# A Fourier filter and a soft mixture of experts on one core: the first DFT stage folded into sums and differences of token pairs, on quarters of PE

## The chip, the cores and the metric

The kernel runs on one core of a Trainium2 chip. The metric is the device time of one execution in microseconds (us). The engines are PE (matrix products; PEld is its weight load), DVE, ACT and POOL (elementwise work; ACT also functions) and SP, which here issues nearly all DMAs. All arrays are float32. float32r is a reduced form of float32 in which a product makes fewer passes over PE.

## The reference

`x` has 8 batches of 2496 tokens and 256 channels. Each batch is filtered along the tokens, and the result goes through a soft mixture of 8 experts with 4 slots each.

```
X = np.fft.rfft(x, axis=1);  Y = X * (filt_r + 1j * filt_i)
x = np.fft.irfft(Y, n=2496, axis=1).reshape(19968, 256)
logits = x @ phi                                   # 19968 x 32 slots
d = softmax of logits over the tokens;  slot_input = d.T @ x
slot_out[e] = relu(slot_input[e] @ w1[e]) @ w2[e]  # 8 experts, 256 -> 1024 -> 256
c = softmax of logits over the slots;   out = c @ slot_out
```

## The kernel before

The DFT of length 2496 = 39 x 64 is done by two smaller ones. A token is `(64*s + 39*k) mod 2496`, with s from 0 to 38 and k from 0 to 63. The **first stage** is the real DFT of length 39 over s, for every k. Of it 20 cosine rows and 20 sine rows are kept. The **second stage** is a complex DFT of length 64 over k, for each of the 20 frequencies.

The host lays x out so that three k stand on the partitions at a time: 3 x 39 = 117 rows, and 22 columns of three k. A *unit* (`b`, `u`) of the first stage is two of those columns, 512 numbers a row; a batch has 11 units. `split_x` makes a rounded copy of the unit (`xh`, a cast to float32r on ACT, line 310) and what the rounding left (`xl`, a subtraction on POOL, line 311). `s1_unit` forms three float32r products on the whole array, `xh` with the rounded weights `w1h`, `xh` with the weights' rest `w1l`, and `xl` with `w1h` (line 327), 120 rows out of 117. ACT copies the result to `at` (line 331), and SP writes `at` to `a_dram` in DRAM (line 284). Batch 0 goes another way (`b < FB`): one float32 product a unit (line 323), without a split.

`load_ash` reads `a_dram` back with k on the partitions, two frequencies at a time (`ash`, 256 KB); a batch's first `ash` needs all of its writes. The main loop has 80 slots, one for each batch and pair of frequencies `c`. In a slot `x_unit` forms the second stage (line 357, `x`), DVE multiplies by the filter `ff_t` (lines 371 and 372) and adds, with POOL, into `yt` (lines 374 and 375). Two slots later `t_unit` transposes `yt` (line 383, `t`), ACT copies it to `y` (line 385), and after each second slot eight products with phi on 32 columns of PE give `l` (line 394). For groups of one or two batches `chain` runs beside the slots: the inverse DFT of the logits, maxima, exponentials, and the sums over tokens (lines 414 to 616; `s` of line 417 is the sum over tokens, `lg` the logits). After the last slot come the rest of the chains, the experts (lines 910 to 939) and the output (lines 966 to 985).

The units of batches 1 to 7 are spread over the slots: `slot_of` gives each its slot, `split_next` splits one slot ahead and asks for the next part of x (`next_x`, three buffers `xt`), and the first `EARLY` units of batch 1 run before the loop. Within these rules a scheduler fixes the order of instructions on each engine at build time. Each engine runs its own in that order. DMAs from `issue` keep the order of the code up to slot `PIN`.

Of the kernel before, what the change touches and what calls it, by code (L numbers as in the profile page):

```python
# [19 lines left out]
NT = 20  # L20
# [28 lines left out]
AB = 5  # L49
EARLY = 4  # L50
# [10 lines left out]
FIRST = (0, 2, 6, 10, 14, 18, 22)  # L61
# [23 lines left out]
def shape_constants():  # L85
# [46 lines left out]
    put("m1", inverse(b1))  # L132
    put("bh", bh.reshape(P, P))
# [60 lines left out]
def token_layout(x):  # L194

    n = np.array([[[token_of(s, min(PK * i + j, N2 - 1)) for i in range(NI)] for s in range(N1)] for j in range(PK)])
    rows = np.zeros((BATCH, P, NI, DIM), x.dtype)
    rows[:, 0:KR] = x[:, n.reshape(KR, NI)]
    return rows
# [26 lines left out]
def fft_soft_moe(ctx, tc, x, ff, phi, wx, cst, w1q, out):  # L226
# [73 lines left out]

    def split_x(b, u):

        if b < FB:
            xhl[b, u] = x0_t[0:KR, 2 * u : 2 * u + 2, :], None
            return
        c, k = divmod(2 * u, XC)
        xs = xts[b, c][0:KR, k : k + 2, :]
        xh = proda.tile([KR, 2, DIM], F32R, tag="xh", name=f"xh{b}_{u}", bufs=3)
        xl = proda.tile([KR, 2, DIM], F32R, tag="xl", name=f"xl{b}_{u}", bufs=3)
        act.copy(xh, xs)  # L310
        pool_e.tensor_tensor(out=xl, in0=xs, in1=xh.bitcast(F32), op=ALU.subtract)  # L311
        xhl[b, u] = xh, xl
# [3 lines left out]
    def s1_unit(b, u):  # L316
        if u == 0:
            a_dram[b] = scr.tile([N2, QR, DIM], F32, tag="a_dram", name=f"a_dram{b}")
        xh, xl = xhl.pop((b, u))
        ps = ps_s1.tile([QP, 2, DIM], F32, tag="s1", name=f"s1_{b}_{u}")  # L320
        if xl is None:
            at = ypool.tile([QP, 2, DIM], F32, tag="y", name=f"at{b}_{u}")
            behind("pe", pe.matmul(ps, w1q_t, xh, start=True, stop=True))
        else:
            at = proda.tile([QP, 2, DIM], F32, tag="at", name=f"at{b}_{u}", bufs=AB)
            for n, (w, xx) in enumerate(((w1h, xh), (w1l, xh), (w1h, xl))):
                pe.matmul(ps, w, xx, start=(n == 0), stop=(n == 2))  # L327
        if b == 0 and u % 2 == 1:
            dve.tensor_copy(at, ps)
        else:  # L330
            act.copy(at, ps)  # L331
# [682 lines left out]
```

## Time and profile before

| | |
|---|---|
| median of 3 runs | 400.98 us (396.01, 400.98, 401.02) |
| profiled execution | 398.26 us, its span 396.3 us, mean granted PE clock 0.96 |
| busy share of the span | PE 91%, PEld 70%, DVE 67%, ACT 54%, POOL 51% |
| DMA | 109.08 MB, mean 275 GB/s |
| first x product | 27.87 us |
| last copy of the first stage | 227.7 us |
| last x product | 287.5 us |
| experts, output | from 322.5 us; from 341.2 us to the end |

In the profile a group of instructions is named by its line, engine, operation and tiles (`out<-in`), with buffer numbers left out. A float32 product on PE leaves two records, a float32r product or a transpose one. A record's length contains the time in which the next one has already begun, so the pace of PE is read from one start to the next. A row such as `117*120 117x512` means 117 rows and 120 columns of PE in use, and 512 columns streamed. The chain of work that ended last goes 61% of its way over PE, 15% over DVE and 13% over DMAs.

### The profile page before, as it was taken

The page shows a single profiled execution, that of the slowest core. Times are in us where ns is not written, and L with a number is a line of the kernel's source. Part 1 is how long each engine was busy: PE and PEld are TensorE (multiplying, and loading weights), DVE is VectorE, ACT ScalarE, POOL GpSimd, SP SyncE. Part 2 cuts the span into 40 slices and gives each one's busy share as a digit, 9 for nine tenths or more (in the row PEclk, how much of TensorE's full clock was granted, in tenths as well). Part 3 has the DMA queues.
Part 4 walks back from the last instruction along what each step waited for, and adds up shares of the span by engine and source line. Part 5 has one row for each costly group of instructions (what it writes and reads, how often), then busy time and mean ns, then how long its engine had stood idle before and what let it go on. Part 6 is the DMA issues. An engine that isn't in the chain of part 4 may idle for free.

```text
span 396.3 us, 11436 instructions
## 1 busy us (share of the span) xinstructions
PE 362.1 (91%) x4569; PEld 278.9 (70%) x4569; DVE 264.2 (67%) x460; ACT 212.6 (54%) x453; POOL 200.8 (51%) x229
## 2 busy tenths in 40 slices
PE   8967889999999999999998999999999899999960
PEld 2455767887878776887887778888767544777850
DVE  1215998779789973967899355899644653588640
ACT  2356656675666946665675634347235431577430
POOL 0157688797668674856774615663421112361000
PEclk9999999999999999999998999999999999999555
DMA  8999999899889866976897783454529998299997
GB/s 293 316 291 368 395 374 373 288 318 341 261 274 305 288 212 207 291 250 171 283 328 215 200 271 104 130 147 134 170 70 380 364 249 278 111 413 421 418 414 296
DMA packets 54010, 109.08 MB, mean 275 GB/s; under 512 B 5362, under 2 KB 25970, under 8 KB 51782
## 3 DMA queue, kind: packets, MB, share of 16 engines
q1 hardware_dynamic: 53412, 108.01, 80.5%
q8 instruction: 36, 0.59, 0.6%
q10 hardware_dynamic: 546, 0.35, 0.3%
q14 instruction: 16, 0.13, 0.1%
HBM read 65.60 MB, written 42.74 MB: 273 GB/s over the span
## 4 chain that ended last, share of the span: by engine, by line
PE 61%; DVE 15%; DMA 13%; ACT 3%; issue 3%; POOL 2%; SPq 1%; DVEq 0%; ACTq 0%; POOLq 0%
PE x L357 14%; PE s L327 9%; PE t L383 7%; DMA out<-ob 5%; PE l L394 4%; PE s L417 4%; DMA ff_t<-in_ff 3%; DMA xt<-in_x 3%; PE v L417 3%; PE dd L417 2%; DVE t L372 2%; PE u L417 2%; PE lg L417 2%; DVE yt L371 2%; DVE yt L374 2%
## 5 line engine op out<-in xcount | busy, mean ns | idle before, releaser
L311 POOL TENSOR_TENSOR xl<-xt,xh 117x512 fp32r<-117x512 f32 x77 | 104.4, 1367 | 37.6 <-ACT xh L310 35.5
L357 PE MATMUL x<-cst_t,ash 128*128 128x128 f32 x640 | 90.2, 281 | 2.9 <-issue 2.3
L357 PEld LDWEIGHTS x<-cst_t,ash 128*128 128x128 f32 x640 | 81.6, 192 | 13.3 <-issue 7.5
L375 POOL TENSOR_TENSOR yt<-yt,t 128x256 f32<-128x256 f32 x80 | 65.4, 818 | 45.5 <-DVE t L372 35.9
L371 DVE TENSOR_TENSOR yt<-x,ff_t 128x512 f32<-128x512 f32 x80 | 54.7, 683 | 27.4 <-PE x L357 25.3
L385 ACT COPY y<-t 128x512 f32<-128x512 f32 x80 | 46.1, 591 | 35.5 <-PE t L383 33.2
L331 ACT COPY at<-s 120x512 f32<-120x512 f32 x83 | 48.5, 587 | 26.2 <-PE s L327 15.1
L310 ACT CAST xh<-xt 117x512 fp32r<-117x512 f32 x77 | 46.3, 623 | 23.4 <-PE s L327 12.6
L372 DVE TENSOR_TENSOR t<-x,ff_t 128x512 f32<-128x512 f32 x80 | 54.2, 678 | 0.0
L383 PE MATMUL t<-cst_t,yt 128*128 128x128 f32 x320 | 48.8, 277 | 4.8 <-POOL yt L375 4.1
L374 DVE TENSOR_TENSOR yt<-yt,t 128x256 f32<-128x256 f32 x60 | 45.3, 766 | 0.8
L383 PEld LDWEIGHTS t<-cst_t,yt 128*128 128x128 f32 x320 | 36.7, 141 | 12.7 <-POOL yt L375 7.2
L327 PE MATMUL s<-xh,w1h 117*120 117x512 f32 x77 | 35.9, 466 | 3.3 <-ACT at L331 2.1
L966 PE MATMUL out<-so,st 32*128 32x256 f32 x468 | 35.6, 337 | 2.0 <-ACT ob L971 1.0
L966 PEld LDWEIGHTS out<-so,st 32*128 32x128 f32 x468 | 30.7, 222 | 6.2 <-ACT ob L971 3.1
L327 PE MATMUL s<-xl,w1h 117*120 117x512 f32 x77 | 31.7, 416 | 0.3 <-POOL xl L311 0.3
L374 POOL TENSOR_TENSOR yt<-yt,t 128x256 f32<-128x256 f32 x20 | 15.1, 754 | 32.6 <-DVE t L372 19.9
L971 DVE COPY ob<-out 128x512 f32<-128x512 f32 (+1 forms) x40 | 25.0, 669 | 8.5 <-DMA out<-ob 5.5
L327 PE MATMUL s<-xh,w1l 117*120 117x512 f32 x77 | 30.4, 395 | 0.0
L971 ACT COPY ob<-out 128x512 f32<-128x512 f32 (+1 forms) x40 | 21.7, 583 | 14.8 <-DMA out<-ob 7.5
L394 PE MATMUL l<-yt,phi_t 128*32 128x128 f32 x640 | 27.5, 280 | 0.1
L394 PEld LDWEIGHTS l<-yt,phi_t 128*32 128x32 f32 x640 | 15.8, 109 | 9.1 <-issue 4.5
(107 smaller groups left out, 474.0 us busy)
## 6 DMA issues: line engine op xcount, KB each, us to landing
ash<-a_dram SPq DMA_DIRECT2D x80, 256.0 KB
a_dram<-at SPq DMA_DIRECT2D x80, 240.0 KB
xt<-in_x SPq DMA_DIRECT2D x35, 512.0 KB
out<-ob SPq DMA_DIRECT2D x17, 1024.0 KB
w<-in_wx SPq DMA_DIRECT2D x42, 256.0 KB
w<-in_wx SPq DMA_DIRECT2D x6, 512.0 KB
x_t<-in_x SPq DMA_DIRECT2D x5, 512.0 KB
ff_t<-in_ff SPq DMA_DIRECT2D x10, 256.0 KB
```

The costliest lines, as they stand in the source:

```text
L311: pool_e.tensor_tensor(out=xl, in0=xs, in1=xh.bitcast(F32), op=ALU.subtract)
L327: pe.matmul(ps, w, xx, start=(n == 0), stop=(n == 2))
L331: act.copy(at, ps)
L357: pe.matmul(ps[:, 2 * k + dh].rearrange("q r c -> q (r c)"), ash[:, k, dh * P : (dh + 1) * P], C("b1" if t0 + k else "b0"), start=True, st ...
L371: dve.tensor_tensor(out=yt, in0=ps, in1=frv, op=ALU.mult)
L372: dve.tensor_tensor(out=t2, in0=ps[:, :, ::-1, :], in1=fiv, op=ALU.mult)
L374: add.tensor_tensor(out=yt[:, :, 1, :], in0=yt[:, :, 1, :], in1=t2[:, :, 1, :], op=ALU.add)
L375: pool_e.tensor_tensor(out=yt[:, :, 0, :], in0=yt[:, :, 0, :], in1=t2[:, :, 0, :], op=ALU.subtract)
L383: pe.transpose(pt[:, k, dh, :], yt[:, c % 2, 2 * k + dh].rearrange("q r c -> q (r c)"), ident)
L394: pe.matmul(pl[32 * j : 32 * j + 32, :], phi_t[:, dh, :], yt[:, j // 2, 2 * (j % 2) + dh].rearrange("q r c -> q (r c)"), start=(dh == 0), ...
L417: line(pe.matmul(*a, **k))
L966: nc.tensor.matmul(prs[k][:, mm, :], sts[n][q, hs, c0 : c0 + P], so[q, ho], start=(i == 0), stop=(i == 2))
```

## The change

Cosine is even and sine odd in s, so the first stage is now done on sums and differences of the tokens s and 39 - s. The host lays x out in pairs: 20 values of s (the first stands alone), three k, two halves of the partitions (`r`), 64 rows each. The 11 units of a batch are taken in six pieces (`PIECE`): the first unit alone, then two at a time. `fold_x` makes the sums (`eo[:, 0]`, on DVE for even pieces and on POOL for odd ones; on DVE for all of batch 0) and the differences (`eo[:, 1]`, on POOL). `s1_unit` forms four float32 products on quarters of PE, 64 rows by 64 columns: cosines from the sums to columns 0 to 63, sines from the differences to columns 64 to 127, for each half of the rows, into two PSUM tiles. Two copies bring them to `at`. Each piece is written with two DMAs of 60 rows (four in the last piece). `a_dram` has the cosine and sine part outside k, so the second stage's constant has its rows in another order (`a1`). Batch 0 uses the same path, with PSUM tiles of three pools in turn and a `keep_warm` product behind pieces 3 and 4. `EARLY` is now 5 (three pieces), `AB` 4, and x is fetched after every piece.

```diff
-AB = 5
-EARLY = 4
+AB = 4
+EARLY = 5
+PIECE = ((0, 1), (1, 3), (3, 5), (5, 7), (7, 9), (9, 11))
+NU = len(PIECE)
+HR = 20
...
-    k = (b - 1) * NH + u - EARLY
+    k = (b - 1) * NH + PIECE[u][1] - 1 - EARLY
...
-    w1q_t = const.tile([KR, QP], F32, name="w1q_t")
-    act.dma_start(w1q_t, w1q)
-    w1h = const.tile([KR, QP], F32R, name="w1h")
-    w1l = const.tile([KR, QP], F32R, name="w1l")
-    nc.vector.tensor_copy(w1h, w1q_t)
-    nc.vector.tensor_tensor(out=w1l, in0=w1q_t, in1=w1h.bitcast(F32), op=ALU.subtract)
+    w1q_t = const.tile([P, 2, 64], F32, name="w1q_t")
+    act.dma_start(w1q_t.rearrange("q c m -> q (c m)"), w1q)
...
-    def keep_warm(n):
+    def keep_warm(n, w=512):
         for k in range(n):
-            behind("pe", pe.matmul(pw, warm[:, 0:P], warm, start=True, stop=True))
+            behind("pe", pe.matmul(pw[:, 0:w], warm[:, 0:P], warm[:, 0:w], start=True, stop=True))
     def load_x(b, c):
-        t = proda.tile([P, XC, DIM], F32, tag="xt", name=f"xt{b}_{c}", bufs=XB)
-        i0 = c * XC
-        n = min(XC, NI - i0)
-        issue(t[:, 0:n, :], x[b, :, i0 : i0 + n, :])
+        t = proda.tile([P, 2, 2, DIM], F32, tag="xt", name=f"xt{b}_{c}", bufs=XB)
+        lo, hi = PIECE[c]
+        issue(t[:, 0 : hi - lo].rearrange("q u a d -> q (u a) d"), x[b, :, 2 * lo : 2 * hi, :])
         xts[b, c] = t
-    xhl = {}
-    def split_x(b, u):
-        if b < FB:
-            xhl[b, u] = x0_t[0:KR, 2 * u : 2 * u + 2, :], None
-            return
-        c, k = divmod(2 * u, XC)
-        xs = xts[b, c][0:KR, k : k + 2, :]
-        xh = proda.tile([KR, 2, DIM], F32R, tag="xh", name=f"xh{b}_{u}", bufs=3)
-        xl = proda.tile([KR, 2, DIM], F32R, tag="xl", name=f"xl{b}_{u}", bufs=3)
-        act.copy(xh, xs)
-        pool_e.tensor_tensor(out=xl, in0=xs, in1=xh.bitcast(F32), op=ALU.subtract)
-        xhl[b, u] = xh, xl
+    eos = {}
+    def fold_x(b, u):
+        lo, hi = PIECE[u]
+        n = hi - lo
+        xs = x0_t[:, lo:hi] if b < FB else xts.pop((b, u))[:, 0:n]
+        eo = proda.tile([P, 2, 2, DIM], F32, tag="eo", name=f"eo{b}_{u}", bufs=2)
+        first = dve if b < FB or u % 2 == 0 else pool_e
+        first.tensor_tensor(out=eo[:, 0, 0:n], in0=xs[:, :, 0], in1=xs[:, :, 1], op=ALU.add)
+        pool_e.tensor_tensor(out=eo[:, 1, 0:n], in0=xs[:, :, 0], in1=xs[:, :, 1], op=ALU.subtract)
+        eos[b, u] = eo
     a_dram = {}
     def s1_unit(b, u):
         if u == 0:
-            a_dram[b] = scr.tile([N2, QR, DIM], F32, tag="a_dram", name=f"a_dram{b}")
-        xh, xl = xhl.pop((b, u))
-        ps = ps_s1.tile([QP, 2, DIM], F32, tag="s1", name=f"s1_{b}_{u}")
-        if xl is None:
-            at = ypool.tile([QP, 2, DIM], F32, tag="y", name=f"at{b}_{u}")
-            behind("pe", pe.matmul(ps, w1q_t, xh, start=True, stop=True))
-        else:
-            at = proda.tile([QP, 2, DIM], F32, tag="at", name=f"at{b}_{u}", bufs=AB)
-            for n, (w, xx) in enumerate(((w1h, xh), (w1l, xh), (w1h, xl))):
-                pe.matmul(ps, w, xx, start=(n == 0), stop=(n == 2))
-        if b == 0 and u % 2 == 1:
-            dve.tensor_copy(at, ps)
-        else:
-            act.copy(at, ps)
-        k0 = PK * 2 * u
-        if u < NH - 1:
-            issue(a_dram[b][k0 : k0 + 2 * PK].rearrange("(i j) q d -> (j q) i d", j=PK), at)
-        else:
-            issue(a_dram[b][k0 : k0 + PK].rearrange("j q d -> (j q) d"), at[:, 0, :])
-            issue(a_dram[b][k0 + PK], at[0:QR, 1, :])
+            a_dram[b] = scr.tile([2, N2, NT, DIM], F32, tag="a_dram", name=f"a_dram{b}")
+        lo, hi = PIECE[u]
+        n = hi - lo
+        eo = eos.pop((b, u))
+        pool, tag = ((ps_s1, "s1"), (ps_x, "x"), (ps_t, "t"))[u % 3 if b < FB else 0]
+        pss = [pool.tile([P, 2, DIM], F32, tag=tag, name=f"s1_{b}_{u}_{r}") for r in range(2)]
+        if b >= FB:
+            queue.pop("four", None)
+        for c in (1, 0):
+            for r in (1, 0):
+                q = slice(64 * r, 64 * r + 64)
+                ins = pe.matmul(pss[r][64 * c : 64 * c + 64, 0:n], w1q_t[q, c], eo[q, c, 0:n], start=True, stop=True)
+                behind("pe" if b < FB else "four", ins)
+        at = proda.tile([P, 2, 2, DIM], F32, tag="at", name=f"at{b}_{u}", bufs=AB)
+        for r in range(2):
+            copy = dve.tensor_copy if b < FB and u % 2 and r else act.copy
+            copy(at[:, 0:n, r], pss[r][:, 0:n])
+        ka, kb = 2 * PK * lo, min(2 * PK * hi, N2 - N2 % PK)
+        for c in range(2):
+            issue(
+                a_dram[b][c, ka:kb].rearrange("(m j) t d -> (j t) m d", j=PK),
+                at[64 * c : 64 * c + PK * HR, 0:n].rearrange("q u r d -> q (u r) d")[:, 0 : (kb - ka) // PK],
+            )
+        if hi == NH:
+            for c in range(2):
+                issue(a_dram[b][c, N2 - 1], at[64 * c : 64 * c + HR, n - 1, 1])
...
-        issue(ash, a_dram[b].rearrange("k (r t) d -> (k r) t d", t=NT)[:, t0 : t0 + 2, :])
+        issue(ash, a_dram[b].rearrange("r k t d -> (r k) t d")[:, t0 : t0 + 2, :])
...
-                    C("b1" if t0 + k else "b0"),
+                    C("a1" if t0 + k else "b0"),
...
-            split_x(b, u)
-            if u % 2 == 1 or u == NH - 1:
-                next_x()
+            fold_x(b, u)
+            next_x()
...
-    split_x(0, 0)
-    for u in range(NH):
-        if u + 1 < NH:
-            split_x(0, u + 1)
+    fold_x(0, 0)
+    for u in range(NU):
+        if u + 1 < NU:
+            fold_x(0, u + 1)
         s1_unit(0, u)
-        if u in (3, 7):
+        if 2 < u < NU - 1:
+            keep_warm(1, 256)
+        if u in (2, 4):
             next_x()
+        if u == 1:
+            tc.keep_in_program_order(act.dma_start(cst_t[:, 0:NEAR], cst[:, 0:NEAR]))
         if u == 2:
-            tc.keep_in_program_order(act.dma_start(cst_t[:, 0:NEAR], cst[:, 0:NEAR]))
-        if u == 4:
             tc.keep_in_program_order(act.dma_start(phi_t, phi.rearrange("(h q) e -> q h e", q=P)))
...
-    for u in range(EARLY):
-        split_x(1, u)
+    for u in range(NEARLY):
+        fold_x(1, u)
         s1_unit(1, u)
-        if u % 2 == 1:
-            next_x()
-            load_to(-2 + u // 2)
+        next_x()
+        if u:
+            load_to(-3 + u)
```

Three places show what the scheduler makes of it. A tile of the first stage's result is called `s_`, batch, unit (or piece), and in the changed kernel the half `r`; the last number is a buffer's. The first is PE's row in the middle of batch 2, before: units 2 and 3, 8 rows.

```order
L327 MATMUL s_2_2_597<-xh_2_535,w1h 120x512
L327 MATMUL s_2_2_597<-xh_2_535,w1l 120x512
L327 MATMUL s_2_3_604<-xh_3_539,w1h 120x512
L327 MATMUL s_2_3_604<-xh_3_539,w1l 120x512
L414 MATMUL ltr_0_1120<-cst_t,lt_406 128x128
L327 MATMUL s_2_2_597<-xl_2_536,w1h 120x512
L357 MATMUL x_7_545<-cst_t,ash_7_418 128x128 x4
L327 MATMUL s_2_3_604<-xl_3_540,w1h 120x512
```

Every product there uses the whole array. In the changed kernel the same place of PE's row holds piece 2 of batch 2 (units 3 and 4):

```order
L369 MATMUL x_8_577<-cst_t,ash_8_458 128x128 x4
L335 MATMUL s_2_2_1_613<-eo_2_572,w1q_t 64x512
L335 MATMUL s_2_2_0_612<-eo_2_572,w1q_t 64x512
L335 MATMUL s_2_2_1_613<-eo_2_572,w1q_t 64x512
L335 MATMUL s_2_2_0_612<-eo_2_572,w1q_t 64x512
L395 MATMUL t_6_588<-cst_t,yt_6_515 128x128 x4
```

Here the four quarters (two of the differences, then two of the sums) stand together between two whole-array products. Of the 42 pieces of batches 1 to 7, 25 stand so (22 of two units, 3 of one). Piece 3 of the same batch, a little later on PE:

```order
L395 MATMUL t_7_623<-cst_t,yt_6_515 128x128 x4
L335 MATMUL s_2_3_1_654<-eo_3_597,w1q_t 64x512
L369 MATMUL x_0_642<-cst_t,ash_0_528 128x128 x4
L335 MATMUL s_2_3_0_653<-eo_3_597,w1q_t 64x512
L335 MATMUL s_2_3_1_654<-eo_3_597,w1q_t 64x512
L335 MATMUL s_2_3_0_653<-eo_3_597,w1q_t 64x512
L406 MATMUL l_3_630<-yt_6_515,phi_t 32x128 x8
```

Here four whole-array products of x have come between the first quarter and the other three. 17 pieces are cut like this: 12 of two units and 4 of one unit in two parts, one of two units in three. Counted over the whole program, PE's row falls into 168 stretches of one tile shape before (whole array, 32 columns, 32 or 64 rows) and into 279 now.

The last place is POOL, batch 2, before:

```order
L311 TENSOR_TENSOR xl_2_536<-xt_1_380,xh_2_535 117x512
L311 TENSOR_TENSOR xl_3_540<-xt_1_380,xh_3_539 117x512
L375 TENSOR_TENSOR yt_6_511<-yt_6_511,t_0_6_510 128x4x64
L311 TENSOR_TENSOR xl_4_583<-xt_2_425,xh_4_582 117x512
L311 TENSOR_TENSOR xl_5_621<-xt_2_425,xh_5_620 117x512
L375 TENSOR_TENSOR yt_6_511<-yt_6_511,t_0_7_550 128x4x64
```

and now:

```order
L316 TENSOR_TENSOR eo_1_504<-xt_1_335 128x512
L317 TENSOR_TENSOR eo_1_504<-xt_1_335 128x512
L387 TENSOR_TENSOR yt_4_432<-yt_4_432,t_0_4_431 128x4x64
L387 TENSOR_TENSOR yt_4_432<-yt_4_432,t_0_5_466 128x4x64
L317 TENSOR_TENSOR eo_2_572<-xt_2_387 128x512
L387 TENSOR_TENSOR yt_6_515<-yt_6_515,t_0_6_514 128x4x64
```

Where POOL had one operation a unit, it has two for a piece of two units when the piece is odd, and one when it is even. The sum of the even piece (`eo_2`, line 316) stands on DVE among the operations of the second stage. The casts of line 310 are gone from ACT.

More of the change, by code (lines that the diff above doesn't have):

```diff
@@ L60 @@
 PIN = 24
-FIRST = (0, 2, 6, 10, 14, 18, 22)
 PA = 6
@@ L118, in shape_constants @@
     w1f = w1.reshape(N1, QR)
-    w1q = np.zeros((PK, N1, PK, QR))
+    fold = np.zeros((2, HR, 2, NT))
+    fold[0, :, 0] = w1[0:HR, 0]
+    fold[1, 1:, 1] = w1[1:HR, 1]
+    w1q = np.zeros((2, 64, 2, 64))
     w1d = np.zeros((PK, N1, 2, PK, 2, NT // 2))
@@ L122, in shape_constants @@
     for j in range(PK):
-        w1q[j, :, j] = w1f
+        sl = slice(HR * j, HR * j + HR)
+        w1q[:, sl, 0, sl] = fold[0, :, 0]
+        w1q[:, sl, 1, sl] = fold[1, :, 1]
         cq[j, :, j] = w1f.T
         w1d[j, :, :, j] = w1.reshape(N1, 2, 2, NT // 2).transpose(0, 2, 1, 3)
-    w1q = w1q.reshape(KR, QP)
-    put("b0", b0.reshape(P, P))
-    put("b1", b1.reshape(P, P))
+    w1q = w1q.reshape(P, P)
+    put("b0", b0.transpose(1, 0, 2, 3).reshape(P, P))
+    put("a1", b1.transpose(1, 0, 2, 3).reshape(P, P))
     put("id", np.eye(P))
@@ L132, in shape_constants @@
     put("m1", inverse(b1))
+    put("b1", b1.reshape(P, P))
     put("bh", bh.reshape(P, P))
@@ L194, in token_layout @@
 def token_layout(x):
[L196 to L199, printed above, removed]
+    rows = np.zeros((BATCH, 2, 64, NH, 2, DIM), x.dtype)
+    for u in range(NH):
+        for k in range(PK * 2 * u, min(PK * 2 * (u + 1), N2)):
+            r, j = divmod(k - PK * 2 * u, PK)
+            for s in range(HR):
+                rows[:, r, HR * j + s, u, 0] = x[:, token_of(s, k)]
+                if s:
+                    rows[:, r, HR * j + s, u, 1] = x[:, token_of(N1 - s, k)]
+    return rows.reshape(BATCH, P, NI, DIM)
 def out_place(m):
@@ L667, in fft_soft_moe @@
     NS = BATCH * CPB
-    units = [(b, u) for b in range(1, BATCH) for u in range(NH)]
+    units = [(b, u) for b in range(1, BATCH) for u in range(NU)]
+    NEARLY = sum(hi <= EARLY for _, hi in PIECE)
     at_slot = {}
-    for b, u in units[EARLY:]:
+    for b, u in units[NEARLY:]:
         at_slot.setdefault(slot_of(b, u), []).append((b, u))
@@ L680, in split_next @@
         for b, u in at_slot.get(n, ()):
-            split_x(b, u)
-            if u % 2 == 1 or u == NH - 1:
-                next_x()
-    x0_t = x0p.tile([P, NI, DIM], F32, name="x0_t")
-    for i0, i1 in zip(FIRST, FIRST[1:]):
-        issue(x0_t[:, i0:i1], x[0, :, i0:i1])
+            fold_x(b, u)
+            next_x()
+    x0_t = x0p.tile([P, NH, 2, DIM], F32, name="x0_t")
+    for lo, hi in PIECE:
+        issue(x0_t[:, lo:hi].rearrange("q u a d -> q (u a) d"), x[0, :, 2 * lo : 2 * hi])
     warm = ypool.tile([P, 512], F32, tag="y", name="warm")
@@ L714, in load_to @@
             b, c = loads[0]
-            if n < max(b * CPB + c - (3 if b < 2 else ASH), slot_of(b, NH - 1) + 2 if b else -3):
+            if n < max(b * CPB + c - (3 if b < 2 else ASH), slot_of(b, NU - 1) + 2 if b else -3):
                 break
```

## The prediction, made before the changed kernel was run

> **What bounds the kernel now.** I read the stretches first: one row per 20 or 40 us, with the busy time of each engine, the granted clock, the DMA share and GB/s.
>
> ```profile
> 0.00:20.00 20.00, 18.14 (x38) 7.28 (x39) 4.46 (x9) 6.22 (x11) 2.11 (x6) 1.00 0.90 305
> 20.00:40.00 20.00, 14.21 (x92) 10.42 (x92) 7.40 (x12) 11.78 (x24) 13.51 (x12) 1.00 0.96 331
> 40.00:60.00 20.00, 17.52 (x151) 13.69 (x150) 18.13 (x25) 12.13 (x25) 15.15 (x14) 1.00 1.03 384
> 60.00:100.00 40.00, 38.64 (x476) 31.99 (x478) 32.31 (x50) 26.93 (x55) 34.34 (x32) 1.00 0.97 327
> 100.00:140.00 40.00, 39.14 (x520) 32.51 (x511) 36.55 (x55) 29.41 (x63) 28.29 (x27) 1.00 0.86 274
> 140.00:180.00 40.00, 39.41 (x533) 31.77 (x533) 26.92 (x43) 23.70 (x48) 25.95 (x25) 1.00 0.77 243
> 180.00:220.00 40.00, 37.66 (x459) 30.86 (x458) 35.80 (x59) 24.96 (x54) 26.94 (x25) 0.96 0.80 249
> 220.00:260.00 40.00, 40.00 (x568) 31.80 (x567) 23.03 (x41) 19.31 (x38) 19.89 (x26) 1.00 0.58 173
> ```
>
> The order of the columns is PE, PEld, DVE, ACT, POOL. Until 60 us the 16 DMA engines are full (0.90 to 1.03) and PE stands idle 8.3 of the 40 us from 20 to 60. From 60 to 260 us PE is busy 194.9 of 200 us: 5.1 us idle in all. So from 60 us on, what the first stage adds to or takes from PE's queue moves the end almost one to one. ACT and POOL have room (29 and 34 of 40 at most); DVE has little from 100 to 140 and from 180 to 220 (3.5 and 4.2 us idle). The groups give the prices of what goes and comes on those engines (busy us and mean ns of one behind the bar):
>
> ```profile
> L311 POOL TENSOR_TENSOR xl<-xt,xh 117x512 fp32r<-117x512 f32 x77 | 104.4, 1367 | 37.6 <-ACT xh L310 35.5 <-PE s L327 1.6 <-DMA a_dram<-at 0.4
> L310 ACT CAST xh<-xt 117x512 fp32r<-117x512 f32 x77 | 46.3, 623 | 23.4 <-PE s L327 12.6 <-DMA xt<-in_x 4.6 <-POOL xl L311 4.3
> L331 ACT COPY at<-s 120x512 f32<-120x512 f32 x83 | 48.5, 587 | 26.2 <-PE s L327 15.1 <-PE s L323 10.0 <-ACT dd L573 0.3
> L371 DVE TENSOR_TENSOR yt<-x,ff_t 128x512 f32<-128x512 f32 x80 | 54.7, 683 | 27.4 <-PE x L357 25.3 <-PE l L394 1.9
> L573 ACT COPY dd<-dd 128x256 f32<-128x256 f32 x3 | 1.1, 377 | 0.7 <-PE dd L417 0.7
> ```
>
> **PE, what goes.** PE's own timeline, in a stretch without waits (start, length, what). Lengths overlap, so only starts count:
>
> ```profile
> 156.05 0.39 PE L327 MATMUL s<-xh,w1l 117*120 117x512 f32 x1
> 156.28 0.39 PE L327 MATMUL s<-xl,w1h 117*120 117x512 f32 x1
> ...
> 156.98 0.39 PE L327 MATMUL s<-xl,w1h 117*120 117x512 f32 x1
> 157.21 0.71 PE L414 MATMUL ltr<-cst_t,lt 128*128 128x128 f32 x5
> 157.76 0.60 PE L383 MATMUL t<-cst_t,yt 128*128 128x128 f32 x4
> 158.29 0.64 PE L394 MATMUL l<-yt,phi_t 128*32 128x128 f32 x16
> 158.86 2.05 PE L357 MATMUL x<-cst_t,ash 128*128 128x128 f32 x16
> ```
>
> From 156.05 to 156.98 four products start, 0.2325 us each. Batches 1 to 7 have 77 units of three: 231 x 0.2325 = **53.7 us** go.
>
> **PE, what comes.** A float32 product of 512 columns on the whole array, and four records of x, as the chain counts them (start, share of the path):
>
> ```profile
> 109.02 0.86 PE lg L417 x2
> 109.88 0.45 PE x L357 x4
> ```
>
> That is 0.86 us a product, 0.43 for 256 columns (a float32 product is two records). Do four quarters run at once? The trace has no 64 by 64 product. It has products on quarters of the columns and on quarters of the rows:
>
> ```profile
> 150.45 4.50 PE L417 MATMUL s<-y,dd 128*32 128x256 f32 x80
> 154.77 0.62 PE L394 MATMUL l<-yt,phi_t 128*32 128x128 f32 x16
> ...
> 359.40 2.76 PE L966 MATMUL out<-so,st 32*128 32x256 f32 x48
> ```
>
> The 80 records of s (256 columns, 0.215 each if alone, 17.2 in all) take 4.32 us from start to start: four at once, in float32. The 48 records of out (float32r, half of 0.2325 each, 5.6 alone) take 2.76: two at once at least, with new weights before each. So I take four quarters at once: a stretch of quarters lasts as long as one of them, 0.86 us, or 0.43 for the one-unit piece. The other end is one after the other, four times that.
>
> By the order of the changed program, the 42 pieces of batches 1 to 7 do not stand whole. Of 35 two-unit pieces 22 are whole, 12 cut in two and one in three; of seven one-unit pieces 3 are whole and 4 cut. A cut piece pays its full length in each part, since the quarter left alone streams as long as four: 22 + 24 + 3 = 49 lengths of 0.86 and 3 + 8 = 11 of 0.43, **46.9 us** come.
>
> **PE, changes of tile shape.** In the rows above, four transposes take 0.43 us when another whole-array product follows, but 0.53 (157.76 to 158.29) when l follows, which uses 32 columns: 0.10 to enter. l's 16 records, four at once, are worth 4 x 0.11 = 0.44, but x starts 0.57 after l: 0.13. And the first eight records of x after l:
>
> ```profile
> 59.05 1.16 PE L357 MATMUL x<-cst_t,ash 128*128 128x128 f32 x8
> 60.05 0.27 PE L414 MATMUL ltr<-cst_t,lt 128*128 128x128 f32 x1
> ```
>
> 1.00 us instead of 8 x 0.111 = 0.89: 0.11 more, in which the first weights load uncovered. In and out together 0.34 us, 0.17 a change. The old first stage has the whole array's shape and pays none: its neighbours follow at 0.23. The new one adds, beside six in batch 0, 105 changes (168 stretches of one shape before, 279 now): **17.9 us**. For 64 by 64 the price is bounded by 0.10 (transposes next, weights hidden) and 0.24 a change; I keep the middle.
>
> Sum on PE: 46.9 + 17.9 - 53.7 = **+11.1 us**. A whole two-unit piece costs 1.20 instead of 1.40; one cut in two costs 2.40. Batch 1's pieces (five stretches: 4.7 + 1.7 instead of 7.7) run before 60 us, where PE idles, so their 1.3 us gain brings nothing: +12.4 where PE is bound. Of the 5.1 us that PE idles there I let 3.5 take some of it up (bounds 0 and 5.1), because a slower queue finds more of its inputs ready.
>
> In the Trainium skill, "TensorE: Matmul & The Clock Gate", section "Measured speedup vs the span model", gives a packed group the length of one product plus about 4 ns per further tile, and no price for changing the shape. By it the changes would cost nothing and the sum would be -6.8. The rows above speak against the missing price; its result is my second case.
>
> **The other engines.** ACT loses 77 casts, 46.3 us, and its copies stay: 70 of 0.587 and 14 of 0.377 instead of 77. POOL has 42 differences and 21 sums, 56 of 512 columns at about 1.29 us and 7 of 256, instead of 77 of 1.367: some 25 us less. Both have room already, so I cost this at nothing. DVE gets 21 sums, 14 of 512 columns. Its like in the trace is the add of L374 at half that size, min/median/max:
>
> ```profile
> L374 DVE TENSOR_TENSOR yt<-yt,t x60: 403/628/1495, 30.7 to 236.1; 128x256 f32<-128x256 f32 x60
> ```
>
> It reads two SBUF operands while POOL works, and 403 ns become up to 1495; L371, with one operand in PSUM, holds 683. A sum of 512 columns lies between 0.68 and 1.8 us; I take 1.0, nearest to the median with 0.3 more for the width: 14 x 1.0 + 7 x 0.63 = 18 us in 200, or 3.7 in 40: that is what DVE has left in its two full stretches, and it hides there as long as a sum takes no longer. Behind a late sum wait the four products, and on PE's queue everything behind these. Bounds 0 and 8 us; I take 0. SP issues two writes of 60 rows instead of one of 120 per two units, the same 2.6 MB a batch: nothing, at worst 1 us at the start. The x loads move the same bytes.
>
> **The start.** The chain of before:
>
> ```profile
> 11.72 5.66 DMA xt<-in_x
> 17.40 1.14 ACT xh L310 x2
> 18.54 0.49 ACT at L331
> ...
> 20.34 5.30 DMA xt<-in_x
> ```
>
> The last copy of batch 0 stands on ACT behind two casts of batch 1 that wait for a load until 17.40; its writes are issued by 20.3, and the first ash is issued only after they land:
>
> ```profile
> 24.07 0.33 SPq L284 DMA_DIRECT2D ash<-a_dram  x1
> 27.87 1.16 PE L357 MATMUL x<-cst_t,ash 128*128 128x128 f32 x8 [0.59 <-DMA ash<-a_dram]
> ```
>
> Now no cast stands there. The last piece of batch 0 (2.8 MB at 305 GB/s) is there at about 10.3 us. With POOL's 1.29, 0.86 on PE, 0.69 for the copy, 1.3 of issues and the same 3.8 to land, ash goes at 18.3; if POOL and DVE take turns, at 2.0 us a piece from 3.9 on, at 22.6: 5.8 or 1.5 us earlier. The full DMA engines from 20 to 60 us take part of it back, all of it at worst. I take **-2.5**.
>
> Sum: 12.4 - 3.5 - 2.5 = +6.4 us on the profiled execution's own 398.26 us (span 396.3), which lies 0.7% under the median 400.98: **405 us**. From 290 us on nothing changes.
>
> **The rivals.**
> - Changes of shape cost little, because they fall into waits: -6.8 on PE, start -2.5 or more, so 386 to 391 us. For it: the sum of lengths does fall. Against: PE has only 5.1 us of waits to hide 17.9 in. 0.17.
> - DVE and POOL become the bound. From 100 to 140 and from 180 to 220 us DVE has 7.7 us left, and the eight or so sums there at 1.0 to 1.8 us take 8 to 14 and hold PE's queue: 405 + 8 = 413, up to 419. It decides once a sum takes over 1 us there. For it: 1495 ns at half the size. Against: POOL works 25 us less beside it. 0.18. The Trainium skill, "GPSIMD Engine Reference", section "1. Specifications", states that VectorE and GPSIMD share their SBUF interfaces and that a DVE instruction with two SBUF inputs contends; the L374 spread agrees, and by it alone each sum would take up to POOL's 1.29 us longer.
> - The quarters do not run at once, at least not two in one band of rows: some 33 us more, 438; none at once, 42 pieces at four lengths, 490. Against: the rows of s and out. 0.05.
> - All is taken up: waits and start return the 11 us: 396 to 400. 0.10.
> - The forecast, 400 to 411: 0.50.
>
> **Chances.** Two per cent (393 to 409 around the median) is about what a measurement of this kernel can tell from no change. Below 393 lies the first rival and little else: 0.18. Above 409: the second, the third and the upper part of the forecast: 0.29. Within: 0.53. The range runs from 390, most of the way into the first rival, to 418, the second; it leaves out about 0.2.
>
> **What would show it.** Records of s on 64 rows and 64 columns should start four together, a whole piece taking about 0.9 us from its first start to the next product's, plus 0.1 to 0.2; cut pieces should show one quarter alone for 0.86. The stretches from 60 to 260 us should have PE at 39 of 40 still, with x units ever later than before (about 7 us at 230 us), and the first x at 25 us. I am wrong if whole pieces take 1.7 us or more (rows in turn), if the s products wait for eo, or if shape changes take under 0.05.

## The result, and the profile after

The changed kernel takes **419.06 us** (median; 417.69 to 419.25, and one disturbed run of 427.16, which the ratio leaves out), beside 400.65 us for the kernel before: ratio 1.0476, 95% interval 1.0377 to 1.0575. The forecast was 405 us with a range from 390 to 418. The profiled execution took 419.25 us, its span 417.4 us, 21.1 more than that of the profiled execution before; the medians lie 18.4 us apart. What follows accounts for the two profiled executions.

The stretches after (PE, PEld, DVE, ACT, POOL, granted clock, DMA share, GB/s), over the same times as those shown of before:

```profile
0.00:20.00 20.00, 15.07 (x62) 4.32 (x63) 7.56 (x12) 6.03 (x11) 10.36 (x11) 1.00 0.85 278
20.00:40.00 20.00, 13.15 (x78) 7.38 (x77) 6.40 (x8) 5.83 (x12) 9.40 (x7) 0.74 0.93 287
40.00:60.00 20.00, 15.35 (x138) 9.83 (x134) 16.79 (x26) 6.27 (x14) 11.68 (x12) 1.00 1.01 362
60.00:100.00 40.00, 38.33 (x353) 24.70 (x352) 34.54 (x54) 17.41 (x38) 29.66 (x28) 1.00 0.98 321
100.00:140.00 40.00, 38.15 (x568) 25.54 (x569) 29.45 (x50) 18.82 (x39) 21.83 (x22) 1.00 0.80 248
140.00:180.00 40.00, 37.84 (x456) 24.75 (x445) 28.88 (x49) 17.75 (x41) 20.58 (x20) 1.00 0.69 203
180.00:220.00 40.00, 37.97 (x611) 25.67 (x610) 32.92 (x57) 19.89 (x44) 20.79 (x20) 1.00 0.80 242
220.00:260.00 40.00, 40.00 (x408) 26.23 (x410) 26.66 (x46) 15.63 (x35) 21.64 (x23) 0.96 0.66 188
```

PE stays the bound from 60 us on, though its idle time there rises from 5.1 to 7.7 us. Until 60 us all is later: PE idles 16.4 us instead of 10.1, its clock is down to 0.74 from 20 to 40 us, and the DMA engines move less. DVE, ACT and POOL have room.

Stretches of equal time hold different work in the two kernels. So I cut both at the same two events: the start of x_1_5 (batch 1, sixth x unit) and that of the last x unit. Before, then after:

```profile
0.00:75.02 75.02, 64.28 (x410) 43.09 (x411) 42.49 (x66) 40.29 (x78) 43.22 (x42) 1.00 0.98 346
75.02:286.75 211.73, 206.45 (x2842) 168.75 (x2841) 164.66 (x267) 126.47 (x263) 135.44 (x136) 0.99 0.74 232
286.75:396.30 109.55, 91.38 (x1319) 67.06 (x1317) 57.04 (x129) 45.87 (x112) 22.16 (x52) 0.87 0.84 311
```

```profile
0.00:80.00 80.00, 62.82 (x429) 33.47 (x429) 49.71 (x72) 27.06 (x55) 46.94 (x45) 0.94 0.94 314
80.00:305.94 225.94, 217.73 (x2958) 152.36 (x2958) 168.06 (x283) 101.75 (x219) 120.99 (x126) 0.99 0.73 221
305.94:417.40 111.46, 94.64 (x1319) 71.06 (x1317) 57.32 (x129) 46.62 (x112) 22.16 (x52) 0.82 0.82 305
```

This is the account of the 21.1 us. x_1_5 starts **5.0 us** later. From there to the end PE is busy 312.4 us instead of 297.8, **+14.5**, and idle 25.0 instead of 23.4, **+1.6**. The forecast had -2.5, +12.4 and -3.5.

The last rows split this further. Behind the last x unit no product of the first stage is left, and both kernels run the same 1319 PE records there; yet PE is busy 3.3 us longer, and the stretch lasts 1.9 us longer, at a granted clock of 0.82 instead of 0.87. The first stage's part of the busy time is therefore 11.3 us, between x_1_5 and the last x unit, where idle time rises by 2.9 us. With one profile of each kernel, whether the change lowered the clock at the end is not shown.

In each experiment below I read the same three numbers; the last three columns are the start of x_1_5, and PE's busy and idle time from there to the end (us):

| kernel | median | ratio to before (95%) | x_1_5 | busy | idle |
|---|---|---|---|---|---|
| before | 398.7 to 401.0 | 1 | 75.0 | 297.8 | 23.4 |
| after | 419.1 | 1.048 (1.038 to 1.058) | 80.0 | 312.4 | 25.0 |
| whole | 414.7 | 1.036 (1.031 to 1.042) | 78.3 | 298.0 | 35.2 |
| whole_ash_first | 415.1 | 1.037 (1.030 to 1.043) | 78.3 | 301.0 | 34.6 |
| whole_no_fold | 412.6 | 1.032 (1.025 to 1.039) | 78.6 | 297.5 | 33.2 |
| whole2 | 409.9 | 1.028 (1.021 to 1.035) | 81.9 | 299.0 | 26.9 |
| whole2_warm | 412.3 | 1.032 (1.026 to 1.039) | 84.0 | 299.4 | 26.2 |
| whole2_late | 425.0 | 1.066 (1.059 to 1.074) | 82.9 | 311.8 | 29.5 |
| whole2_act | 408.4 | 1.025 (1.016 to 1.034) | 78.5 | 300.9 | 26.5 |
| whole2_x_early | 407.4 | 1.020 (1.014 to 1.027) | 77.9 | 301.4 | 26.3 |
| whole2_act_x_early | 408.4 | 1.022 (1.014 to 1.030) | 79.4 | 299.5 | 27.0 |
| whole2_x_early5 | 408.4 | 1.019 (1.007 to 1.031) | 77.3 | 298.7 | 29.6 |
| fp32_on_before | 406.0 | 1.017 (1.010 to 1.025) | 72.2 | 305.2 | 21.1 |
| shapes_on_before | 407.3 | 1.019 (1.013 to 1.025) | 75.3 | 308.4 | 21.4 |

The quarters themselves came as forecast. PE's timeline after, at a whole piece and at a cut one:

```profile
164.71 1.09 PE L335 MATMUL s<-eo,w1q_t 64*64 64x512 f32 x8
165.73 0.66 PE L395 MATMUL t<-cst_t,yt 128*128 128x128 f32 x4
...
167.98 1.07 PE L335 MATMUL s<-eo,w1q_t 64*64 64x512 f32 x2
168.98 0.94 PE L369 MATMUL x<-cst_t,ash 128*128 128x128 f32 x6
169.85 1.08 PE L335 MATMUL s<-eo,w1q_t 64*64 64x512 f32 x6
170.86 0.66 PE L395 MATMUL t<-cst_t,yt 128*128 128x128 f32 x4
```

All eight records of a whole piece last 1.02 us to the next product's start, so four quarters run at once. One quarter alone lasts 1.00 and the other three 1.01: the cut piece pays its length twice. No product waits for the sums (`eo`) in this part: PE's five waits for them, 10.2 us in all, lie before 36 us.

### The profile page after: what moved, and what is told of

It reads as the page before. It is cut to its first block, busy times and chain, and to the rows that moved or that the text cites. A ratio compares the mean times of both kernels' runs of the same rounds, so it can differ in the third digit from the quotient of the medians.

```text
span 417.4 us, 11636 instructions
## 1 busy us (share of the span) xinstructions
PE 375.2 (90%) x4704; PEld 256.9 (62%) x4704; DVE 275.1 (66%) x483; ACT 175.4 (42%) x386; POOL 190.1 (46%) x221
## 3 DMA queue, kind: packets, MB, share of 16 engines
q1 hardware_dynamic: 53612, 108.07, 78.6%
## 4 chain that ended last, share of the span: by engine, by line
PE 70%; DMA 10%; DVE 8%; issue 3%; ACT 2%; SPq 2%; POOL 1%; ACTq 0%; POOLq 0%; DVEq 0%
PE x L369 16%; PE s L335 11%; PE t L395 8%; PE out L980 6%; PE l L406 5%; PE s L429 4%; PE dd L429 3%; DMA xt<-in_x 3%; PE lg L429 3%; PE v L429 2%; DMA ash<-a_dram 2%; SPq L293 2%; PE u L429 2%; PE h L924 2%; PE o L942 2%
## 5 line engine op out<-in xcount | busy, mean ns | idle before, releaser
L369 PE MATMUL x<-cst_t,ash 128*128 128x128 f32 x640 | 94.7, 289 | 7.2 <-DVE t L384 1.7
L340 ACT COPY at<-s 128x512 f32<-128x512 f32 (+1 forms) x93 | 47.5, 551 | 80.2 <-PE s L335 58.3
L335 PE MATMUL s<-eo,w1q_t 64*64 64x512 f32 (+1 forms) x384 | 71.4, 637 | 10.2 <-POOL eo L317 10.2
L317 POOL TENSOR_TENSOR eo<-xt 128x512 f32<-128x512 f32 (+1 forms) x42 | 55.1, 1311 | 14.2 <-DMA xt<-in_x 5.7
L395 PE MATMUL t<-cst_t,yt 128*128 128x128 f32 x320 | 51.6, 285 | 0.0
L386 DVE TENSOR_TENSOR yt<-yt,t 128x256 f32<-128x256 f32 x60 | 41.1, 690 | 0.7
L316 POOL TENSOR_TENSOR eo<-xt 128x512 f32<-128x512 f32 x21 | 27.5, 1308 | 20.2 <-issue 8.7
L980 PEld LDWEIGHTS out<-so,st 32*128 32x128 f32 x468 | 32.8, 253 | 3.6 <-DVE ob L985 1.7
L335 PEld LDWEIGHTS s<-eo,w1q_t 64*64 64x64 f32 x384 | 14.0, 142 | 27.4 <-POOL eo L317 17.3
L316 DVE TENSOR_TENSOR eo<-xt 128x512 f32<-128x512 f32 (+1 forms) x21 | 17.9, 854 | 18.1 <-DMA xt<-in_x 16.1
L406 PEld LDWEIGHTS l<-yt,phi_t 128*32 128x32 f32 x640 | 15.7, 109 | 13.8 <-issue 10.7
```

What stands on the lines that cost most here:

```text
L317: pool_e.tensor_tensor(out=eo[:, 1, 0:n], in0=xs[:, :, 0], in1=xs[:, :, 1], op=ALU.subtract)
L335: ins = pe.matmul(pss[r][64 * c : 64 * c + 64, 0:n], w1q_t[q, c], eo[q, c, 0:n], start=True, stop=True)
L340: copy(at[:, 0:n, r], pss[r][:, 0:n])
L369: pe.matmul(ps[:, 2 * k + dh].rearrange("q r c -> q (r c)"), ash[:, k, dh * P : (dh + 1) * P], C("a1" if t0 + k else "b0"), start=True, st ...
L386: add.tensor_tensor(out=yt[:, :, 1, :], in0=yt[:, :, 1, :], in1=t2[:, :, 1, :], op=ALU.add)
L395: pe.transpose(pt[:, k, dh, :], yt[:, c % 2, 2 * k + dh].rearrange("q r c -> q (r c)"), ident)
```

## The experiments

**Cut pieces.** Theory: 14.5 us of PE's time are lengths and changes of tile shape, and most of it is the 17 cut pieces. Rival: PE waits for the sums anyway.

```diff
+    class Whole:                       # all of PE's instructions go through it
+        def _do(self, f, a, k):
+            ins = f(*a, **k)
+            if four:                   # the fourth quarter of the last piece
+                tc.add_manual_dep(ins.ins, four[-1].ins.name, info, reason="order of issue")
+            seen.append(ins)
+            return ins
...
+                    if (c, r) == (1, 1):
+                        for o in seen[-13:-1]:
+                            tc.add_manual_dep(ins.ins, o.ins.name, info, reason="order of issue")
```

> The changed kernel with the four quarters of every piece kept together in PE's order (no other product between them); nothing else changed. The stretches of one tile shape fall from 279 to 237 and the 17 cut pieces become whole. Theory 1 (the cuts and the shape changes carry the loss): 14 lengths of 0.86, 4 of 0.43 and 42 changes of 0.17 go, 20.9 us, all of it in the part where PE is bound: 396 to 402 us. Rival (the four products wait for the sums of POOL and DVE, and PE's queue stands behind them): PE gives its gain back as waiting time, 410 us or more.

414.66 us: PE's busy time falls by 14.4 us, to that of before, but its idle time rises by 10.2. The time is the rival's, the wait is not: the new idle time stands at the chain of the logits (whole, PE's waits from 78 to 308 us: sum, times, longest; L247 is the helper's line):

```profile
PE mt L247 <- DVE cmax L538: 5.7, 2, 2.9
PE v L247 <- issue: 2.5, 1, 2.5
```

The tie holds products of this chain, which wait for DVE and ACT, in front of pieces that could run. So I tied only x products and transposes (the edit against the changed kernel, shortened).

```diff
+    def after_four(ins):               # tie to the fourth quarter of the last piece
...
+                if b >= FB and (c, r) == (1, 1) and last_x:
+                    tc.add_manual_dep(ins.ins, last_x[-1].ins.name, info, reason="order of issue")
...
+                last_x.append(after_four(ins))
...
-                pe.transpose(
+                after_four(pe.transpose(
```

> The changed kernel with 40 of 42 pieces whole (the x products traced before a piece stand ahead of it, the x products and transposes traced later behind it), but without the first kernel of whole pieces' tie on the chain of the logits (mt, mb, u, v), behind whose waits PE stood 15.0 us there. Theory (cut pieces cost PE 0.86 us and two shape changes each; the tie alone took the gain back): PE's waits at mt and mb go, and the time is 400 to 408 us. Rival (PE waits as long elsewhere, whatever the order, since the sums, the loads of ash or DVE are the bound): 412 us or more, as with the tie.

409.89 us, a little above what the theory allowed: 9.2 less than the changed kernel. Busy falls by 13.4 us with 15 of the 17 cuts gone; idle is 1.9 above the changed kernel's, and x_1_5 another 1.9 later. Cut pieces are thus about half of the loss (9.2 of 18.4 us between the medians), and even whole pieces bring no gain: busy 299.0, against 297.8 before.

**The sums.** This kernel leaves the sums and differences out of whole for batches 1 to 7:

```diff
+        if b >= FB:
+            eos[b, u] = xs.rearrange("q u a d -> q a u d")
+            return
-XB = 3
+XB = 5
```

> The kernel with whole pieces, and for batches 1 to 7 without the sums and differences: the products read the loaded tokens themselves (the result is that of unfolded tokens), with five buffers for the loads instead of three and two for the sums. POOL loses 56 passes and DVE 21. If PE's waits for the sums cost time (17.3 us of waiting by the weight loads and 10.2 by the products in the changed kernel), the time falls by 5 to 15 us against whole pieces alone. If those waits only fill time that another wait would fill, it stays within 3 us.

-2.0 us against whole pieces (412.62 and 414.66, their intervals overlap): the rival. PE then waits for the loads instead of the sums. DVE or POOL as the bound falls with it.

**Length and shape by themselves, on the kernel before.**

```diff
+            if u % 2 == 0:
+                pe.matmul(ps[0:64, 0, 0:4], ident[0:64, 0:64], ident[0:64, 0:4], start=True, stop=True)
```

> The kernel before, with a product of 64 by 64 and 4 columns ahead of the three products of every other unit of batches 1 to 7 (42 of them; its output is overwritten by the unit's own products): the stretches of one tile shape rise from 168 to 246, nothing else changes. At 0.17 us a change (the forecast's price): 78 x 0.17 = 13.3 us and about 1 us for the products, 410 to 417 us. If changes of tile shape cost next to nothing (the first rival): 400 to 404 us.

407.28 us, 1.3 to 2.5% slower: the first rival falls, and the size lies under the forecast's 410. Between x_1_5 and the last x unit PE's busy time rises by 9.0 us (215.4 for 206.5) for 54 more changes (counted in the trace), 0.17 each with the small products in it, and 1.0 us of idle time takes part of it up. The scheduler's order changed with the edit, too: the last product of the first stage stands behind 65 x units, and behind 60 before.

Now length alone:

```diff
-        xh, xl = (casts and differences as before)
+        xhl[b, u] = xs, None      # one float32 product of 512 columns
-XB = 3
+XB = 6
```

> The kernel before, with one float32 product of the whole array for each unit of batches 1 to 7 instead of three float32r ones (as its batch 0 has), without the casts on ACT and the differences on POOL; six buffers for the loads instead of three. No change of tile shape is added. Lengths: 77 x 0.86 = 66.2 us instead of 53.7, so 12.5 us more on PE, of which 10.7 from 60 us on. If length alone counts and PE passes it on: 410 to 414 us. If the step from x to a float32 product costs more than that to a float32r one (x before a float32r product is 0.08 us short, before a quarter 0.10 long), 66 steps at some 0.2 come on top: 420 us or more. If PE's idle time takes it up: 405 us or less.

406.01 us, between the two expectations. In the profiled execution 7.3 of the 10.7 us come, idle time takes up 2.4, and the start gains 2.8: x_1_5 at 72.2 us. But this execution took 400.23 us, the others 405.64 us or more: the trace accounts for 2.1 us, and the rest of the median's 6 us stays open. A whole-array float32 product has no seam: x ends 5 ns late before it, 98 ns late before a quarter, and 77 ns early before a float32r product (medians of starts between records, beyond 0.111 us for each x record). The float32r product gives that back: it takes 0.318 us to the next start, against 0.233 within a run of them.

**The start.** SP's issues in the kernel before, then after:

```profile
11.72 0.61 SPq L284 DMA_DIRECT2D xt<-in_x  x1
...
16.30 0.68 SPq L284 DMA_DIRECT2D xt<-in_x  x1
...
26.43 1.28 SPq L284 DMA_DIRECT2D ash<-a_dram  x1
```

```profile
14.11 0.80 SPq L293 DMA_DIRECT2D xt<-in_x  x1
...
18.56 0.99 SPq L293 DMA_DIRECT2D xt<-in_x  x1
...
25.77 0.33 SPq L293 DMA_DIRECT2D ash<-a_dram  x1
...
31.92 1.30 SPq L293 DMA_DIRECT2D ash<-a_dram  x1
```

Batch 1's first two loads are issued 2.4 and 2.3 us later (and the first is half as large now), since batch 0's writes stand ahead of them and wait for folded pieces; the second ash load is 5.5 us later, behind writes of batch 1. The late load then holds up batch 0 itself. Its last copy stands on DVE behind batch 1's first sum, which waits for that load:

```profile
18.50 0.42 DVE L316 TENSOR_TENSOR eo<-xt 128x256 f32<-128x256 f32 x1 [2.65 <-DMA xt<-in_x]
18.85 0.68 DVE L340 COPY at<-s 128x512 f32<-128x512 f32 x1
```

ACT copies the other half of the same piece from 18.04 us. PE meets this as waits, and x_0_1 (37.57 us; 33.27 before) stands in PE's queue behind a piece that waits:

```profile
27.09 1.98 PE L335 MATMUL s<-eo,w1q_t 64*64 64x512 f32 x8 [4.31 <-POOL eo L317]
29.24 2.07 PE L369 MATMUL x<-cst_t,ash 128*128 128x128 f32 x8 [0.17 <-DMA ash<-a_dram]
...
35.28 1.45 PE L335 MATMUL s<-eo,w1q_t 64*64 64x512 f32 x8 [2.37 <-POOL eo L317]
...
37.57 1.92 PE L369 MATMUL x<-cst_t,ash 128*128 128x128 f32 x8
```

Six runs each took one suspect. The place of the ash loads:

```diff
+        if u:
+            load_to(-3 + u)
         s1_unit(1, u)
         next_x()
-        if u:
-            load_to(-3 + u)
```

> The kernel with whole pieces, and at the start each load of the first x units issued ahead of the next piece's writes of batch 1 on SP's queue, not behind them. Theory (the start was lost on SP's queue: x_1_5 started 5.0 us later than before the change instead of 2.5 us earlier): x units 0_1 to 1_5 start 3 to 5 us earlier, and the end follows by 2 to 5 us against whole pieces alone. Rival (the start is bound by the x and table loads that fill the DMA engines): no change within 1.5 us.

No change (415.11, x_1_5 at 78.3): the rival. The clock:

```diff
         fold_x(1, u)
+        keep_warm((0, 0, 4, 2)[u])
         s1_unit(1, u)
```

> The kernel of whole2 with six more products of 512 columns that only keep PE busy: four ahead of batch 1's third piece, two ahead of its fourth, where PE waited 4.3 and 2.4 us for POOL's differences in the changed kernel. Theory (those gaps bring PE's clock to half from 25.8 to 32.6 us and from 36.0 to 39.4 us, and the start loses by it): the granted clock from 20 to 40 us rises from 0.74 to 0.9 or more, x_1_5 starts 2 to 4 us earlier, and the end follows. Rival (x and table loads bound the start, the clock does not matter): within 1 us of whole2.

The clock from 20 to 40 us went from 0.63 in whole2 to 0.83, but x_1_5 came 2.1 us later, as the added products stood in the way of the third piece (x_0_0 at 35.1 us, not 31.1). So the start is not won back this way, and what the slow clock costs by itself stays open. Fewer pieces of batch 1 ahead:

```diff
-EARLY = 5
+EARLY = 3
```

> The kernel of whole2 with two of batch 1's pieces ahead of the first x unit instead of three (3 units instead of 5), and each later piece two units later against the x units. 33 pieces are whole instead of 40, so some 9 us of lengths and changes come back, as in the changed kernel. Theory (the start is lost because x units stand on PE's and SP's queues behind pieces of batch 1 that wait for their loads): x_1_5 starts at 78 us or earlier instead of 81.9, by which 4 us of the 9 are won back: 411 to 416 us. Rival (the start is lost before the first x unit, in batch 0's own stage and its writes): x_1_5 within 1 us of 81.9.

x_1_5 at 82.9: the theory falls. The time is worse than either expected: busy rises by 12.8 us for seven pieces more that are cut, not 9. The trace has 6.5 us of lengths and 22 changes of shape more from x_1_5 to the last x unit; the rest is not settled. Batch 0's writes on two queues:

```diff
-            issue(
+            (issue if b >= FB or c == 0 else act.dma_start)(
                 a_dram[b][c, ka:kb]...
```

> The kernel of whole2 with half of batch 0's writes of the first stage (the differences' half of each piece) issued on ACT's queue instead of SP's; SP has seven DMA issues less before the first load of ash. Theory (SP issues without a pause from 14.1 to 23.3 us in the changed kernel, since each piece has two writes, and the first ash load waits for the last of them): the first ash load is issued 2 us or more earlier, at 24 us or before, and x_0_0 with it, and the time falls by 1 to 4 us against whole2. Rival (batch 0's products and sums are late themselves, or the DMA engines are full): the first ash load moves by less than 1 us, no change of the time within 1.5 us.

The first ash load goes at 24.52 instead of 24.63 us, so the mechanism named is refuted: batch 0's last copy on DVE starts at 18.40 us, again behind batch 1's first sum, and not before (17.90 in whole2). Yet x_1_5 comes 3.4 us earlier, and why is not shown. The median, -1.5 us, cannot be told from none. The early x loads:

```diff
+        if u < 3:
+            next_x()
         s1_unit(0, u)
-        if u in (2, 4):
-            next_x()
...
     keep_warm(WK)
-    next_x()
```

> The kernel of whole2 with batch 1's first three x loads issued on SP right behind batch 0's own (ahead of batch 0's writes, behind which the second and third stood and were issued at 18.6 and 22.3 us in the changed kernel). Theory (the start is lost because SP's queue holds these loads back, so that the DMA engines carry 11.3 MB by 40 us instead of 12.7 before the change): 12 MB or more by 40 us, x_0_1 and x_1_5 start 3 us or more earlier than in whole2 (36.6 and 81.9), and the time falls by 2 to 5 us to 405 to 408. Rival (the loads then only delay batch 0's writes and the first ash loads): x_0_0 later than 31.1, and no gain by x_1_5 beyond 1 us.

13.0 MB are moved by 40 us (before 12.7, after 11.3, whole2 11.8), x_0_0 starts at 25.6 and x_1_5 at 77.9 instead of 81.9: the theory, by its own numbers, except that x_0_1 gains 2.4 us and not 3. The gain begins in batch 0: its last DVE copy no longer stands behind a sum that waits (16.61 us instead of 17.90), and the first ash load is issued at 22.32 instead of 24.63. The median falls by 2.5 us, to 407.36; the intervals of the two ratios overlap.

Then this and the ACT queue together:

> Both changes of the start at once on whole2: the early x loads, and half of batch 0's writes on ACT's queue. Theory: x_1_5 at 77 us or earlier, and a time of 403 to 407 us, the fastest of the folded kernels, but not faster than the kernel before, since the x units and transposes around the pieces stay longer on PE and the chain of the logits keeps its waits. Rival: the two overlap fully, 408 to 410 us.

408.37 us: the two overlap fully, the rival. And five buffers:

```diff
-XB = 3
+XB = 5
-        if u < 3:
+        if u < 4:
             next_x()
```

> The kernel of whole2_x_early with five buffers for the x loads instead of three, and the fourth load of batch 1 (that of its piece of units 5 and 6) also ahead of batch 0's last writes. In whole2_x_early x_0_0 started at 25.6 us and x_0_1 at 34.2, since PE stood 5.5 us before that piece, which waited for POOL's difference and this for its load, and x_0_1 stands behind it on PE. Theory (the start is a matter of when these loads are issued): that wait falls to 2 us or less, x_0_1 starts at 31.5 us or earlier, x_1_5 at 76 or earlier instead of 77.9, and the time is 404 to 407 us. Rival (the bytes that come earlier only push back the ash and table loads): x_1_5 at 77.5 or later, 407 us or more.

PE's first waits in whole2_x_early and in this kernel:

```profile
25.57 1.16 PE L381 MATMUL x<-cst_t,ash 128*128 128x128 f32 x8
32.26 1.99 PE L343 MATMUL s<-eo,w1q_t 64*64 64x512 f32 x8 [5.54 <-POOL eo L325]
34.17 3.63 PE L381 MATMUL x<-cst_t,ash 128*128 128x128 f32 x16
```

```profile
27.23 1.16 PE L381 MATMUL x<-cst_t,ash 128*128 128x128 f32 x8 [0.22 <-DMA ash<-a_dram]
36.38 2.08 PE L381 MATMUL x<-cst_t,ash 128*128 128x128 f32 x8 [6.96 <-DMA ash<-a_dram]
```

The wait for the difference goes, and one of 6.96 us for the ash load takes its place; x_1_5 at 77.3 and 408.39 us answer mostly to the rival. That the loads compete by then is my reading, not tested. What keeps x_1_5 2.3 us behind the kernel before stays open.

No version beats the kernel before; the fastest folded one, whole2_x_early, is 1.4 to 2.7% slower.

## Why the prediction was wrong, by its own steps

- **Four quarters at once: right.** 1.02 us for a whole piece, 1.00 for a quarter alone, against "about 0.9, plus 0.1 to 0.2" and 0.86. The rival of 438 to 490 us is out.
- **Lengths and cuts: right in kind.** Undoing 15 cuts takes 13.4 us off PE's busy time. That cut pieces lose what whole ones win stood in the sum.
- **Changes of shape: about right.** Between x_1_5 and the last x unit the pieces of batches 3 to 7 run. Lengths make -4.4 us there (33.5 for 37.9), so 15.7 us (11.3 and 4.4) fall on 81 more changes: 0.19 each; the test on the kernel before gave 0.17, the forecast's price. The seams agree: a whole piece's 1.02 us for 0.86, 0.09 us for the last x or transpose ahead of it and 0.05 to 0.10 for the first behind it make 0.31 to 0.36 for two changes. The Trainium skill, "TensorE: Matmul & The Clock Gate", section "Measured speedup vs the span model", names no such price; the runs show one, and decide.
- **"Of the 5.1 us that PE idles there I let 3.5 take some of it up": wrong, about 6 us.** From 60 to 260 us idle time rose by 2.6, and between x_1_5 and the last x unit by 2.9. In the two runs on the kernel before it fell by 1.0 and 1.9 us in that stretch, never by 3.5. What decides the sign is not shown: the scheduler's order changed in those two runs as well (the last product of the first stage behind 65 and 64 x units, behind 64 in the changed kernel, and behind 60 before). What the traces show is that the chain of the logits meets PE at other places. PE's waits after, 80 to 306 us:

```profile
PE u L429 <- ACT u L567: 4.5, 3, 2.0
PE v L429 <- issue: 1.7, 1, 1.7
PE x L369 <- DVE t L384: 0.9, 1, 0.9
```

- Before, u's wait for ACT was 0.7 us there. whole, whole2 and the changed kernel have 17.0, 10.0 and 8.2 us of idle time between x_1_5 and the last x unit. Their edits differ in the order alone, so the order can move this term by 9 us, more than the whole sum of the forecast.
- **"The start ... I take -2.5": wrong, 7.5 us**, half of the miss. The first ash load went 1.7 us later (25.77 for 24.07), not earlier, and the first x unit started at 29.24 us, not at 25. "Now no cast stands there" was the step that failed. Batch 1's first sum stands there instead, on DVE ahead of batch 0's last copy, and waits for its load until 18.50 us. And the casts had cost little: without them and without sums (fp32_on_before) the last copy on ACT starts at 17.38 us instead of 18.45, and the first ash load goes 0.6 us earlier. The step's slower sum, 22.6 us, did count the turns of POOL and DVE, and POOL ended in time (15.31 us for about 15.9); PE, the copy, the issues and the landing then took 1.6, 1.1, 0.6 and 0.6 us more than their terms.
- The step also ended at the first ash load. It left out that each piece of batch 1 waits for POOL, that POOL waits for loads that are issued later, and that x units on PE are queued behind these pieces: at x_0_1 4.3 of the 5.0 us were lost, before any piece of batch 2. The early loads won 4.0 of whole2's 6.9 us back; the rest stays open. The bound of 0 on that term was too narrow as well: "The full DMA engines take part of it back, all of it at worst".
- **"From 290 us on nothing changes": wrong, 1.9 us.** The work is the same, but behind the last x unit the clock is at half for 40.2 us instead of 28.0, with one such span of 3.4 us at 326 us that the kernel before does not have. Its cause stays open.
- **DVE and POOL: cost at nothing, right after the start.**

```profile
L316 DVE TENSOR_TENSOR eo<-xt x21: 411/693/1750, 18.5 to 244.2; 128x512 f32<-128x512 f32 x14, 128x256 f32<-128x256 f32 x7
L317 POOL TENSOR_TENSOR eo<-xt x42: 732/1276/1791, 18.5 to 250.2; 128x512 f32<-128x512 f32 x35, 128x256 f32<-128x256 f32 x7
```

- A sum of 512 columns on DVE takes 0.69 us in the median and up to 1.75, within the bounds of 0.68 and 1.8; taking all of them away from whole brought 2.0 us. The second rival's time of 413 to 419 was near the result by luck: its mechanism, sums that hold PE's queue from 100 us on, was not there. The Trainium skill, "GPSIMD Engine Reference", section "1. Specifications", has a DVE instruction with two SBUF inputs contend with GPSIMD. The trace agrees, and shows who pays. Nine of the 21 sums took over 0.9 us, and ahead of each an operation of POOL had begun. In six others, of 512 columns, the sum began 0.04 to 0.10 us ahead of POOL's difference and kept 0.69 us; the difference then took 1.72 to 1.79 us instead of 1.27.
- Sum on the profiled execution: +5.0 (start) + 11.3 (busy) + 2.9 (idle) + 1.9 (behind the last x unit) = 21.1 us, for -2.5 + 12.4 - 3.5 + 0 = 6.4. The cut at x_1_5 puts batch 2's pieces into the start, while the forecast had them in its 12.4, so single terms compare only roughly.

## What to carry to other kernels

Splitting a product over tiles saves length only if the tiles stay together in the engine's order and the neighbours share their shape: count the stretches in the built order, and price each change on the path. A new stage ahead of a product lengthens the pipe's fill, where nothing hides it; follow there every queue that its loads, sums and writes share with older work, in order, not only the last item. When work moves in an in-order queue, assume that other waits grow until shown otherwise: idle time took up 1.0 and 1.9 us of extra length in two kernels here and grew by 2.9 in the third. And compare the stretch behind the change too: the same work can run there at another clock.

## What the runs showed of the hardware

A wait of 4.31 us on PE is paid twice: the eight records of s behind it take 1.98 us instead of 1.09, and the clock stays at half for 6.8 us in the changed kernel's start. The Trainium skill, "TensorE: Matmul & The Clock Gate", section "What's actually happening", has an idle window of about 3.4 us halve the clock; the traces agree (half-clock spans of 3.4 and 6.8 us). The kernel whole, with 17.0 us of waits between x_1_5 and the last x unit, fell to half three times there, 17.1 us in all. And what follows a product sets when the next can start: the last x record takes 0.205 us to the next start when a quarter follows, 0.112 when a whole-array float32 product does, and 0.031 when a float32r product does, which then takes 0.085 us longer itself.
